# A two-stage Fourier filter and a gated MLP on one core: another order of loads and work in the first batch

## The chip, the cores and the metric

The kernel runs on one core of one Trainium2 chip. The metric is the device time of one execution in microseconds (us). The time before is the median of nine executions. One execution was also recorded by the hardware profiler; "the page" is the summary of that record, and "the trace" is the record itself.

## The reference

```python
def _attn_ref(x, filt_r, filt_i):            # x: (8, 3008, 256)
    X = np.fft.rfft(x, axis=1)
    F = (filt_r + 1j * filt_i)[None, :, :]   # filters: (1505, 256)
    return np.fft.irfft(X * F, n=x.shape[1], axis=1)

def _moe_ref(x, w_in, w_out, beta):          # x: (24064, 256)
    h = x @ w_in                             # w_in: (256, 2048)
    g = h * (1.0 / (1.0 + np.exp(-beta * h)))
    return g @ w_out                         # w_out: (2048, 256)
```

The output of the first part, 8 sequences of 3008 rows, is the input of the second, 24,064 tokens. Inputs and output are float32; the kernel multiplies in bf16.

## The kernel before

**The transform as matmuls.** The length S = 3008 is split as 47 x 64 (N1 = 47, M = 64). A forward transform is two matmul stages with a twiddle between them folded into the second table: table t1 (94 x 96) for the first, t2 (128 partitions x 24 frequencies k x 128) for the second. NK = 24, and each k stands for 64 frequencies (m) and, by symmetry, two rows of real and imaginary part. The inverse uses t3 (128 x 24 x 192, built from t2 by transposes, its last 64 columns negated) and t4 (t1 transposed). All tables are made on the chip from counting patterns (iota) and the sine function of ScalarE. The filters lie in fr_sb and fi_sb, 128 partitions x 24 x 256 in float32: row m of k on partition m and once more on partition 64 + m, so that a whole 128-partition product can be formed.

**The filters' way in.** `load_filters` (L86 to 91) is called for six groups of KU = 4 frequencies. Each call issues four loads on SP's queue of 128 KB each: fr for the first 32 rows (H = 32), fr for the last 32 (these are read backwards in the array), then fi for the same two. fr goes to partitions 64 to 127, fi to partitions 0 to 63. The 24 loads stand behind a two-element load `seen` (L310), which waits for a piece of t2, so that they do not start ahead of the first batch's input x0. `spread` (L470 to 473) then copies, on GpSimd (POOL), one group's fr and fi to the other 64 partitions.

**The first batch** is done ahead of everything, with functions of its own and an order written by hand at L303 to 345 and L475 to 531; the calls follow each other in each engine's queue as they are written:

- `s1_0` (L245) is the first stage with t1, `a0_turn` (L271) transposes its result for one group (it is evacuated by ScalarE or VectorE), `t2_half` and `t2_shift` (L222, L232) fill t2's halves, `t3_part` and `t3_neg` (L288, L294) fill one of three parts of t3, and `spin` (L267) issues matmuls whose result nobody reads.
- `s2_0(u)` (L426) is the second stage for group u: four matmuls into one PSUM buffer of two banks, then two products on VectorE, with fr_sb (L434) and with the sign rot and fi_sb (L435), to the tiles pq0 and pq1 (128 x 1024 bf16, two buffers each).
- `unit(u)` (L459) multiplies the products of group u by t3 (`s3_0`, L439) and lets ScalarE evacuate into zT. Group 5 goes by `s3_0` and `z_evac` to both engines.
- `z_turn`, `f4`, `f4_head`, `f4_tail` (L396 to 420) are turns of zT and the last stage with t4, which give y; here only for the first 512 tokens. The rest comes later, inside the MLP (`z_late`, `f_late`, L630 and L633).

All two-bank PSUM buffers of this part come from one pool of three.

**POOL's queue at this point** (L475 to 486) is, in this order: four spreads, the load of win_sb (the 1 MB of input weights, converted to bf16 on the way, one DMA), two spreads, the four loads of batch 1's input (xg, `load_x`), two scalings of output weights (`scale_wout`, L373). SP's queue has the filter loads and then the first two loads of output weights (ws, `load_wout`, L365).

**The MLP** (L751 to 791) runs 752 steps, 47 blocks of 512 tokens by 16 pieces of 128 hidden columns. A step issues two matmuls with win_sb into hps (L761), the Silu on ScalarE (L770), whatever a plan has put at this step (`at`, L642), and the four output matmuls of two steps earlier (L779). The plan (L663 to 711) spreads the transforms of batches 1 to 7 over the steps. For batch 1 it begins at once: `z_late` at steps 0 and 1, the sixteen first-stage pieces from step 0 on, two every three steps, each with a matmul on xg (L552), `f_late` for the second 512 tokens of batch 0 at steps 11, 11, 12 and 13, and the load of the stage's result (`a2_load`) at step 13.

Of the kernel before, what the change touches and what calls it, by code (L numbers as in the profile page):

```python
# [10 lines left out]
P = 128  # L11
# [25 lines left out]
def kernel(  # L37
# [45 lines left out]
    WZ = KP * J  # L83
    CH = M * J

    def load_filters(k0, k1):  # L86
        n = k1 - k0
        for filt, dst, p0 in ((filt_r, fr_sb, M), (filt_i, fi_sb, 0)):
            for q0, off, sg in ((p0, k0, 1), (p0 + H, N1 - k0, -1)):
                src = AP(filt.tensor, filt.offset + off * D, [[N1 * D, H], [sg * D, n], [1, D]])  # L90
                nc.sync.dma_start(dst[q0 : q0 + H, k0:k1, :], src)  # L91

    t1 = consts.tile([NP, KP], BF16, name="t1", tag="t1")
    t4 = consts.tile([KP, NP], BF16, name="t4", tag="t4")
# [46 lines left out]
    def iota(tile_, pattern, base=0, ch=0):  # L141
        nc.gpsimd.iota(tile_, pattern=pattern, base=base, channel_multiplier=ch)
# [39 lines left out]
    iota(kc[:], [[1, NK], [0, 2]])  # L182
    iota(cc[:], [[0, NK], [1, 2]], base=1)
    load_x0(8, 16)
    iota(vi[:, :, :H], [[1, NK], [N1, H]])
    load_x0(16, 24)
    iota(vi[:, :, H:], [[1, NK], [-N1, H]], base=N1 * (M - 1))
    load_x0(24, 28)
    make_identity(nc, ident)
    load_x0(28, 32)  # L190
# [2 lines left out]
    def shift_and(name, sh, mask, eng=None):  # L193
        t = small(name, I32)
        eng = eng or nc.vector
        if sh:
            eng.tensor_scalar(t[:], ip[:], sh, mask, ALU.logical_shift_right, ALU.bitwise_and)
        else:
            eng.tensor_scalar(t[:], ip[:], mask, None, ALU.bitwise_and)
        return t  # L200

    def affine(name, src, mul, add, eng=None):
        t = small(name)
        (eng or nc.vector).tensor_scalar(t[:], src[:], mul, add, ALU.mult, ALU.add)
        return t
# [10 lines left out]
    ms = affine("ms", shift_and("m_i", 0, M - 1), TURN / S, 0.0)  # L216
    off = affine("off", c_i, -TURN / 4, TURN / 4)
    q_i = shift_and("q_i", 0, 1)
    v_i = shift_and("v_i", 5, 1)
    q_p = (affine("q0", q_i, -1.0, 1.0), affine("q1", q_i, 1.0, 0.0))  # L220

    def t2_half(hi):  # L222
        t = sq.tile([P, NK, H], I32, name="u", tag=f"u{hi}")
        nc.vector.tensor_scalar(  # L224
            t[:], vi[:, :, hi * H : (hi + 1) * H], ms[:], off[:], ALU.mult, ALU.add
        )
        fold(t[:])
        nc.scalar.activation(
            t2[:, :, hi * H : (hi + 1) * H], t[:], ACT.Sin, scale=TWO_PI / TURN
        )  # L230

    def t2_shift(hi):  # L232
        for c in range(2):
            d0, s0 = (0, M) if c == 0 else (M, 0)
            dst = t2[d0 : d0 + M, :, M + hi * H : M + (hi + 1) * H]
            src = t2[s0 : s0 + M, :, hi * H : (hi + 1) * H]
            if c == hi:
                nc.vector.tensor_scalar_mul(dst, src, -1.0)
            else:
                nc.vector.tensor_copy(dst, src)  # L240

    MG = 4
    aTv = aT[:].rearrange("p e k (g m) -> p g e k m", m=MG)
# [20 lines left out]

    idle = tpsum.tile([P, 512], F32, name="tps", tag="tps")

    def spin(n):  # L267
        for _ in range(n):
            nc.tensor.matmul(idle[:], lhsT=rest[:, :P], rhs=rest[:], start=True, stop=True)

# [23 lines left out]
    def t3_neg(g, on_act):  # L294
        ks = slice(g * KH, (g + 1) * KH)
        evac(t3[:, ks, P:], t3[:, ks, :M], on_act, -1.0)
# [3 lines left out]
        nc.tensor.transpose(tp[:KP, 0, :NP], t1[:], ident[:NP, :NP])  # L300
        nc.scalar.activation(t4[:], tp[:KP, 0, :NP], ACT.Copy)

    spin(15)  # L303
    t1v = t1[:].rearrange("p (k q) -> p k q", q=2)
    for q in range(2):
        nc.scalar.activation(t1v[:, :, q], sn[:NP], ACT.Copy, scale=q_p[q][:NP])
# [1 line left out]
    t2_half(1)  # L308
    seen = sp.tile([1, 2], BF16, name="seen", tag="seen")
    nc.sync.dma_start(seen[:], t2[:1, 1, M - 2 : M])  # L310
    for u in range(NUN):
        load_filters(u * KU, (u + 1) * KU)
    gp = nc.gpsimd
    rot = affine("rot", v_i, 2.0, -1.0, gp)
    tiny = sp.tile([P, NFB], F32, name="tiny", tag="tiny")
    gp.tensor_tensor(tiny[:], beta_sb[:], beta_sb[:], ALU.mult)
    gp.tensor_scalar(tiny[:], tiny[:], 1e-12, 2e-6, ALU.is_lt, ALU.mult)
    gp.tensor_tensor(beta_sb[:], tiny[:], beta_sb[:], ALU.add)
    s1_0(0, (False,))
    s1_0(1, (True,))  # L320
    spin(5)
    t2_shift(0)
    t2_shift(1)
    nc.vector.memset(t2[:, 0, M : P : M - 1], 0.0)
    nc.scalar.activation(warm[:], ms[:], ACT.Silu)
    s1_0(2, (False,))
    s1_0(3, (True,))
    turn_t4()
    nc.gpsimd.tensor_scalar(t4[0:4], t4[0:4], 0.5, None, ALU.mult)
    spin(5)  # L330
    s1_0(4, (False,))
    s1_0(5, (True,))
    t3_part(0, True)
    s1_0(6, (False,))
    spin(2)
    s1_0(7, (False, True))
    spin(2)
    a0_turn(0, [turn8(), bank2([P, KH, P], BF16)], (False, True))
    a0_turn(1)
    t3_neg(0, False)  # L340
# [19 lines left out]
    def load_x(b, g):  # L360
        t = xpool.tile([KP, JG, D], BF16, name="xg", tag="xg")
        load_rows(t[:], b, g * JG, (g + 1) * JG)
        xg[b, g] = t
# [59 lines left out]
    r_p0 = ExitStack()  # L423
    p0pool = rpool("p0pool", r_p0, bufs=2, **tw)

    def s2_0(u):  # L426
        ps = bank2([P, KU, D])
        for i in range(KU):
            k1 = u * KU + i
            nc.tensor.matmul(ps[:, i, :], lhsT=t2[:, k1, :], rhs=a0[:, k1, :], start=True, stop=True)  # L430
        ks = slice(u * KU, (u + 1) * KU)
        for c in range(2):
            pq[u, c] = p0pool.tile([P, KU, D], BF16, name="pq_t", tag=f"pq{c}")
        nc.vector.tensor_tensor(pq[u, 0][:], ps[:], fr_sb[:, ks, :], ALU.mult)  # L434
        nc.vector.scalar_tensor_tensor(  # L435
            pq[u, 1][:], ps[:], rot[:], fi_sb[:, ks, :], ALU.mult, ALU.mult
        )
# [32 lines left out]
    def spread(u):  # L470
        ks = slice(u * KU, (u + 1) * KU)
        nc.gpsimd.tensor_copy(fr_sb[:M, ks, :], fr_sb[M:, ks, :])  # L472
        nc.gpsimd.tensor_copy(fi_sb[M:, ks, :], fi_sb[:M, ks, :])  # L473

    for u in range(4):  # L475
        spread(u)
    nc.gpsimd.dma_start(win_sb[:], moe_w_in.rearrange("(dc p) f -> p dc f", p=P))
    spread(4)
    spread(5)
    for g in range(4):  # L480
        load_x(1, g)
    load_wout(0)
    load_wout(WG)
    scale_wout(0)
    scale_wout(WG)

    s2_0(0)
    a0_turn(2)
    s2_0(1)
    unit(0)  # L490
    t3_part(1, True)
    t3_neg(1, True)
    a0_turn(3)
    s2_0(2)
    unit(1)
    a0_turn(4)
    s2_0(3)
    unit(2)
    a0_turn(5)
    t3_part(2, True)  # L500
    t3_neg(2, True)
    s2_0(4)
    unit(3)
    s2_0(5)
    unit(4)
    banks.close()

# [14 lines left out]
    for e in range(NDC):  # L522
        for h in range(2):
            pool, tag = (lps, "lp") if e else (fps, "fp")
            ps = pool.tile([P, 4, P], F32, name="fp", tag=tag)
            f4(0, h, e, ps)
            f4_head(0, h, e, ps, h == 1)
            late.append((0, h, e, ps))
    for a in late:
        f4_tail(*a, False)  # L530
    tail.close()
# [131 lines left out]
    for b in range(1, B):  # L663
        o = first_step[b - 1]
        if b == 1:
            at(0, z_late, 1, 0)
            at(1, z_late, 1, 1)
            s1_steps(1, range(16), [(2 * i + 1) // 3 for i in range(16)], False, (1, 4, 7, 10, 13))
            for i, r in enumerate((11, 11, 12, 13)):
                at(r, f_late, 1, i // 2, i % 2)  # L670
            for g in range(NG):
                at(o + 13, a2_load, 1, g)
            for hh, z0, f0 in ((2, (13, 14), (15, 16, 17, 18)), (3, (18, 19), (20, 21, 22, 23))):
                for e in range(NDC):
                    at(z0[e], z_late, hh, e)
                for i, r in enumerate(f0):
                    at(r, f_late, hh, i // 2, i % 2)
            s23_steps(1, [o + r for r in (22, 24, 26, 28, 30, 34, 36, 38, 40, 42, 44, 46)], 5, 1)
            for h in range(J // JG):
                at(o + 54, zz_load, 1, h)  # L680
            s4_steps(1, [o + 66 + (i * 12) // 15 for i in range(16)], 2)
            for f in (2, 3):
                at(f, load_wout, f * WG)
                at(f, scale_wout, f * WG)
            if B > 2:
                for g in range(4):
                    at(o + 24 + 3 * g, load_x, 2, g)
                late = (54, 55, 56, 57, 58, 59, 60, 61, 66, 67, 68, 70, 72, 73, 74, 76)
                s1_steps(2, range(16), [o + r for r in late], False)
                for g in range(NG):  # L690
                    at(o + 80, a2_load, 2, g)
                if B > 3:
                    for g in range(4):
                        at(o + (62, 68, 88, 92)[g], load_x, 3, g)
            continue
        base = [o + 16 * n + s for n in range(4) for s in (4, 8, 12)]
        if b == 2:
            base[:6] = [o + r for r in (8, 12, 19, 22, 26, 29)]
        s23_steps(b, base, 6, False)
        for h in range(J // JG):  # L700
            at(o + 70, zz_load, b, h)
        s4_steps(b, [o + 80 + (i * 13) // 15 for i in range(16)], False)
        if b + 1 < B:
            early = [o + 16 * n + s for n in range(4) for s in (7, 13)]
            late = [o + s for s in (66, 67, 69, 70, 72, 73, 75, 76)]
            s1_steps(b + 1, range(16), early + late, False)
            for g in range(NG):
                at(o + 82, a2_load, b + 1, g)
            if b + 2 < B:
                for g in range(4):  # L710
                    at(o + (30, 62, 88, 92)[g], load_x, b + 2, g)
# [108 lines left out]
```

## Time and profile before

| | us |
|---|---|
| median of nine executions | 783.02 |
| lowest and highest | 782.28, 784.27 |
| the profiled execution | 782.77 |
| its span in the record | 781.0 |
| TensorE busy (share) | 768.3 (98%) |
| ScalarE busy (share) | 552.5 (71%) |
| VectorE busy (share) | 446.5 (57%) |
| POOL busy (share) | 151.0 (19%) |

The profiled execution's own time is 1.77 us above its span, which begins with the first and ends with the last recorded instruction. PE is TensorE, PEld its weight loads, DVE VectorE, ACT ScalarE, SP SyncE. L434 is line 434 of the kernel. In a row of a timeline the first number is the time from the span's start, the second the duration, then engine, line, operation, and written and read tiles with partitions x elements and type; a bracket tells how long the engine stood idle before it and what it waited for. In the chain of waits each row is one step of the chain that ended last. The row of digits shows the busy share in tenths for forty equal slices of the span, 19.5 us each.

### The profile page before, as it was taken

The numbers are of one execution on the slowest core, as the hardware profiler recorded it, in microseconds if no ns is written. First come the engines' busy times: TensorE is split into PE (matmuls) and PEld (weight loads), VectorE is DVE, ScalarE is ACT, GpSimd is POOL, SyncE is SP. The second block draws the span as 40 slices with busy tenths as digits, with TensorE's granted clock in tenths as the row PEclk, the third lists the DMA queues.
The fourth block names the chain that finished last, engine by engine and source line by source line (L and its number), as shares of the span: only waits on it lengthen the run. The fifth ranks groups of instructions, "written<-read, shape, count | busy, mean of one in ns | idle before, by whom it ended". The sixth has DMA issues, their size and how long they took to land.

```text
span 781.0 us, 15238 instructions
## 1 busy us (share of the span) xinstructions
PE 768.3 (98%) x6046; PEld 543.3 (70%) x6046; DVE 446.5 (57%) x713; ACT 552.5 (71%) x814; POOL 151.0 (19%) x154
## 2 busy tenths in 40 slices
PE   8799999999999999999999999999999999999997
PEld 5567767766776667866678666776667776776665
DVE  8869754866556665566646665567655666321001
ACT  6767867666677766777667776677666777777776
POOL 6714400322012220122201322022200222000000
PEclk9999999999999999999999999999999999999999
DMA  9975575244912358042671417622164111500101
GB/s 185 236 225 98 150 204 156 68 104 122 256 39 76 107 111 247 29 106 77 139 220 40 125 48 180 177 75 68 49 189 135 48 48 48 157 28 28 55 28 55
DMA packets 84139, 88.51 MB, mean 113 GB/s; under 512 B 5772, under 2 KB 74380, under 8 KB 84068
## 3 DMA queue, kind: packets, MB, share of 16 engines
q1 hardware_dynamic: 79892, 73.81, 31.6%
q0 software_dynamic: 4032, 13.60, 10.3%
q8 instruction: 47, 0.77, 0.4%
q14 instruction: 24, 0.20, 0.1%
q10 hardware_dynamic: 144, 0.13, 0.0%
HBM read 54.47 MB, written 46.66 MB: 129 GB/s over the span
## 4 chain that ended last, share of the span: by engine, by line
PE 95%; DMA 2%; POOL 1%; DVE 1%; issue 1%; SPq 0%; ACT 0%; DVEq 0%; POOLq 0%
PE acc L779 42%; PE hps L761 42%; PE ps L552 3%; PE ps L620 2%; PE ps L598 2%; PE ps L568 2%; DMA xg<-in_x_dram 1%; DMA fr_sb<-in_filt_r_dram 1%; POOL fi_sb L473 1%; POOL fr_sb L472 1%; PE tp L400 0%; SPq L91 0%; PE ps L405 0%; DVE u L224 0%; DVE u L145 0%
## 5 line engine op out<-in xcount | busy, mean ns | idle before, releaser
L770 ACT ACTIVATE gT<-hps,beta_sb 128x512 bf16<-128x512 f32 x752 | 516.9, 687 | 213.9 <-PE hps L761 212.2
L779 PE MATMUL acc<-wout_sb,gT 128*128 128x256 bf16 x3008 | 453.0, 272 | 0.0
L761 PE MATMUL hps<-y,win_sb 128*128 128x512 bf16 (+7 forms) x1728 | 447.9, 351 | 0.6 <-DMA win_sb<-in_moe_w_in_dram 0.6
L779 PEld LDWEIGHTS <-gT 128*128 128x128 bf16 x3008 | 286.8, 98 | 121.9 <-issue 1.4
L587 POOL TENSOR_TENSOR yh<-a_t,b_t 128x512 bf16<-128x512 f32 x84 | 106.5, 1268 | 422.9 <-DVE b_t L586 421.6
L761 PEld LDWEIGHTS <-win_sb 128*128 128x128 bf16 x1728 | 164.8, 98 | 25.0 <-DMA win_sb<-in_moe_w_in_dram 0.8
L112 DVE COPY ost<-acc 128x512 f32<-128x512 f32 (+1 forms) x94 | 60.0, 680 | 138.3 <-PE acc L779 138.2
L112 DVE CAST a<-ps 96x512 bf16<-96x512 f32 x107 | 72.9, 685 | 52.7 <-PE ps L552 48.7
L114 DVE TENSOR_SCALAR y<-ps 128x376 bf16<-128x376 f32 (+2 forms) x128 | 63.2, 510 | 61.5 <-PE ps L620 57.9
L582 DVE TENSOR_TENSOR a_t<-ps,fr_sb 128x512 f32<-128x512 f32 x84 | 58.1, 692 | 67.0 <-PE ps L568 66.5
L583 DVE SCALAR_TENSOR_TENSOR b_t<-ps,fi_sb 64x512 f32<-64x512 f32 x84 | 58.2, 693 | 1.1
L586 DVE TENSOR_TENSOR b_t<-ps,fi_sb 64x512 f32<-64x512 f32 x84 | 57.4, 683 | 1.1
L112 DVE CAST z<-ps 128x512 bf16<-128x512 f32 x72 | 49.3, 685 | 1.7 <-PE ps L598 0.8
L620 PEld LDWEIGHTS <-zz 96*128 96x128 bf16 x448 | 29.7, 97 | 22.9
L552 PE MATMUL ps<-xg,t 94*96 94x512 bf16 x112 | 42.0, 382 | 0.8 <-DMA xg<-in_x_dram 0.8
L620 PE MATMUL ps<-t,zz 96*128 96x94 bf16 x448 | 34.7, 205 | 0.0
L598 PE MATMUL ps<-yh,t 128*128 128x256 bf16 x168 | 32.1, 273 | 0.0
L568 PE MATMUL ps<-a,t 128*128 128x256 bf16 x168 | 32.1, 273 | 0.0
L598 PEld LDWEIGHTS <-t 128*128 128x128 bf16 x168 | 16.2, 98 | 17.7 <-issue 0.7
L568 PEld LDWEIGHTS <-t 128*128 128x128 bf16 x168 | 16.1, 98 | 16.3
L171 POOL DMA_DIRECT2D xg<-in_x_dram x24 | 12.5, 521 | 56.7 <-PE ps L552 56.7
L552 PEld LDWEIGHTS <-t 94*96 94x96 bf16 x112 | 13.7, 123 | 11.0 <-DMA xg<-in_x_dram 0.9
(94 smaller groups left out, 175.2 us busy)
## 6 DMA issues: line engine op xcount, KB each, us to landing
out_dram<-ost SPq DMA_DIRECT2D x42, 512.0 KB, 3.0
d<-a SPq DMA_DIRECT2D x28, 384.0 KB, 5.2
a<-d SPq DMA_DIRECT2D x28, 384.0 KB, 5.0
d<-z SPq DMA_DIRECT2D x28, 384.0 KB, 3.7
zz<-d SPq DMA_DIRECT2D x28, 384.0 KB, 6.8
xg<-in_x_dram POOLq DMA_DIRECT2D x24, 384.0 KB, 6.2
out_dram<-ost SPq DMA_DIRECT2D x9, 256.0 KB, 3.5
ws<-in_moe_w_out_dram SPq DMA_DIRECT2D x4, 512.0 KB, 6.2
```

The lines of the kernel that those rows point to most:

```text
L112: nc.vector.tensor_copy(dst, src)
L114: nc.vector.tensor_scalar_mul(dst, src, scale)
L552: nc.tensor.matmul(ps[:KP], lhsT=t1[:], rhs=xg[b, g][:NP, jj : jj + 2, :], start=True, stop=True)
L568: nc.tensor.matmul(ps[:, e, :], lhsT=t2[:, k0 + e, :], rhs=st["a2", b, g][:, kk + e, :], start=True, stop=True,)
L582: nc.vector.tensor_tensor(a_t[:], ps[:], fr_sb[:, ks, :], ALU.mult)
L583: nc.vector.scalar_tensor_tensor(b_t[:M], ps[M:], -1.0, fi_sb[M:, ks, :], ALU.mult, ALU.mult)
L587: nc.gpsimd.tensor_tensor(yh[:], a_t[:], b_t[:], ALU.add)
L598: nc.tensor.matmul(ps[:, e, :], lhsT=t3[:, 2 * i + e, :P], rhs=yh[:, e, :], start=True, stop=True)
L620: nc.tensor.matmul(ps[:, e, :NP], lhsT=zz[:, j0 % JG + e, dc * P : (dc + 1) * P], rhs=t4[:], start=True, stop=True,)
L761: nc.tensor.matmul(hps[:, pos - t0 : pos - t0 + ln], lhsT=win_sb[:, dc, fb * P : (fb + 1) * P], rhs=ys[b][:, dc, n0 : n0 + ln], start=(dc ...
L770: nc.scalar.activation(gT[:], hps[:], ACT.Silu, scale=beta_sb[:, fb : fb + 1])
L779: nc.tensor.matmul(acc_of(i, tb)[:, tb % 2, :], lhsT=blk[i * NFB + fb][:, tb * P : (tb + 1) * P], rhs=wout_sb[:, fb, :], start=(fb == 0 an ...
```

## The change

It touches only what happens before the MLP and in its first steps.

- **Filters.** The first and last 32 rows are no longer put side by side in each half of 64 partitions but alternately (even and odd partitions), in the filters and in the columns of t2 (and so of t3). Loads alternate between fr and fi. For k below 16 (DUP) there are 16 loads of 128 KB as before; for k from 16 to 23 there are four loads of 256 KB to the usual halves and four more of 256 KB to the other halves, straight from HBM. The spreads of groups 4 and 5 are gone.
- **Table t2.** Its second 64 columns were made by four operations (two copies, two negations); now by two exclusive-or operations on pairs of bf16 read as int32, which flip the sign of one of the pair. The sign rot comes from the lowest bit of the partition index, not from bit 5; v_i is gone.
- **Group 4's second product** is made on POOL: ScalarE copies the PSUM result, scaled with rot, to zc (float32), and `pool_product` multiplies it with fi_sb in two operations of 128 x 512.
- **Input weights** come in two loads, columns 0 to 511 and the rest, and the first load of xg follows at once. The other three and the two scalings of output weights follow `pool_product(4)` in POOL's queue.
- **Order by hand.** The second part of t3 moves ahead of `unit(0)`, the turns of groups 4 and 5 ahead of `unit(1)` and of `s2_0(4)`, `s2_0(4)` ahead of `unit(2)`, `s2_0(5)` ahead of `unit(3)`. Three idle matmuls are added before `unit(3)`, two before the `f4_tail`s.
- **Plan.** Batch 1's first stage comes two steps later, its `a2_load` one step later, and `f_late` of the second 512 tokens at steps 2 to 5.

```diff
-    def load_filters(k0, k1):
-        n = k1 - k0
-        for filt, dst, p0 in ((filt_r, fr_sb, M), (filt_i, fi_sb, 0)):
-            for q0, off, sg in ((p0, k0, 1), (p0 + H, N1 - k0, -1)):
-                src = AP(filt.tensor, filt.offset + off * D, [[N1 * D, H], [sg * D, n], [1, D]])
-                nc.sync.dma_start(dst[q0 : q0 + H, k0:k1, :], src)
+    FILTERS = ((filt_r, fr_sb), (filt_i, fi_sb))
+    DUP = 2 * KH
+
+    def load_filters(k0, k1, halves):
+        for hi, off, sg in ((0, k0, 1), (1, N1 - k0, -1)):
+            for (filt, dst), p0 in zip(FILTERS, halves):
+                src = AP(filt.tensor, filt.offset + off * D, [[N1 * D, H], [sg * D, k1 - k0], [1, D]])
+                nc.sync.dma_start(dst[p0 + hi : p0 + M : 2, k0:k1, :], src)
...
-    v_i = shift_and("v_i", 5, 1)
...
-    def t2_shift(hi):
-        for c in range(2):
+    def t2_shift():
+        pairs = t2[:].rearrange("p k m -> p (k m)").bitcast(I32).rearrange("p (k m) -> p k m", k=NK)
+        for c, bit in enumerate((1 << 15, -(1 << 31))):
             d0, s0 = (0, M) if c == 0 else (M, 0)
-            dst = t2[d0 : d0 + M, :, M + hi * H : M + (hi + 1) * H]
-            src = t2[s0 : s0 + M, :, hi * H : (hi + 1) * H]
-            if c == hi:
-                nc.vector.tensor_scalar_mul(dst, src, -1.0)
-            else:
-                nc.vector.tensor_copy(dst, src)
+            nc.vector.tensor_scalar(
+                pairs[d0 : d0 + M, :, H:], pairs[s0 : s0 + M, :, :H], bit, None, ALU.bitwise_xor
+            )
...
-    for u in range(NUN):
-        load_filters(u * KU, (u + 1) * KU)
+    for u in range(DUP // KU):
+        load_filters(u * KU, (u + 1) * KU, (M, 0))
+    load_filters(DUP, NK, (M, 0))
+    load_filters(DUP, NK, (0, M))
     gp = nc.gpsimd
-    rot = affine("rot", v_i, 2.0, -1.0, gp)
+    rot = affine("rot", q_i, 2.0, -1.0, gp)
...
-    def s2_0(u):
+    zc = sr.tile([P, KU, D], F32, name="zc", tag="zc")
+
+    def s2_0(u, on_pool=False):
...
+        if on_pool:
+            nc.scalar.activation(zc[:], ps[:], ACT.Copy, scale=rot[:])
         nc.vector.tensor_tensor(pq[u, 0][:], ps[:], fr_sb[:, ks, :], ALU.mult)
+        if on_pool:
+            return
         nc.vector.scalar_tensor_tensor(
             pq[u, 1][:], ps[:], rot[:], fi_sb[:, ks, :], ALU.mult, ALU.mult
         )
...
+    def load_win(f0, f1):
+        nc.gpsimd.dma_start(
+            win_sb[:, :, f0:f1], moe_w_in[:, f0:f1].rearrange("(dc p) f -> p dc f", p=P)
+        )
+
     for u in range(4):
         spread(u)
-    nc.gpsimd.dma_start(win_sb[:], moe_w_in.rearrange("(dc p) f -> p dc f", p=P))
-    spread(4)
-    spread(5)
-    for g in range(4):
-        load_x(1, g)
+    load_win(0, 4 * P)
+    load_win(4 * P, FF)
+    load_x(1, 0)
+
+    def pool_product(u):
+        for i in range(0, KU, 2):
+            k0 = u * KU + i
+            nc.gpsimd.tensor_tensor(
+                pq[u, 1][:, i : i + 2, :], zc[:, i : i + 2, :], fi_sb[:, k0 : k0 + 2, :], ALU.mult
+            )
+
     load_wout(0)
     load_wout(WG)
-    scale_wout(0)
-    scale_wout(WG)
 
     s2_0(0)
     a0_turn(2)
     s2_0(1)
-    unit(0)
     t3_part(1, True)
     t3_neg(1, True)
+    unit(0)
     a0_turn(3)
     s2_0(2)
+    a0_turn(4)
     unit(1)
-    a0_turn(4)
     s2_0(3)
+    a0_turn(5)
+    s2_0(4, True)
+    pool_product(4)
+    for g in range(1, 4):
+        load_x(1, g)
+    scale_wout(0)
+    scale_wout(WG)
     unit(2)
-    a0_turn(5)
     t3_part(2, True)
     t3_neg(2, True)
-    s2_0(4)
+    s2_0(5)
+    idle = tpsum.tile([P, 512], F32, name="tps", tag="tps")
+    spin(3, idle)
     unit(3)
-    s2_0(5)
     unit(4)
...
+    spin(2, zps.tile([P, 512], F32, name="zp", tag="zp"))
     for a in late:
         f4_tail(*a, False)
...
-            s1_steps(1, range(16), [(2 * i + 1) // 3 for i in range(16)], False, (1, 4, 7, 10, 13))
-            for i, r in enumerate((11, 11, 12, 13)):
+            s1_steps(1, range(16), [2 + (2 * i + 1) // 3 for i in range(16)], False, (1, 4, 7, 10, 13))
+            for i, r in enumerate((2, 3, 4, 5)):
                 at(r, f_late, 1, i // 2, i % 2)
             for g in range(NG):
-                at(o + 13, a2_load, 1, g)
+                at(o + 14, a2_load, 1, g)
```

More of the change, by code (lines that the diff above doesn't have):

```diff
@@ L184 @@
     load_x0(8, 16)
-    iota(vi[:, :, :H], [[1, NK], [N1, H]])
+    viv = vi[:].rearrange("p k (m h) -> p k m h", h=2)
+    iota(viv[:, :, :, 0], [[1, NK], [N1, H]])
     load_x0(16, 24)
-    iota(vi[:, :, H:], [[1, NK], [-N1, H]], base=N1 * (M - 1))
+    iota(viv[:, :, :, 1], [[1, NK], [-N1, H]], base=N1 * (M - 1))
     load_x0(24, 28)
@@ L224, in t2_half @@
         nc.vector.tensor_scalar(
-            t[:], vi[:, :, hi * H : (hi + 1) * H], ms[:], off[:], ALU.mult, ALU.add
+            t[:], viv[:, :, :, hi], ms[:], off[:], ALU.mult, ALU.add
         )
@@ L228, in t2_half @@
         nc.scalar.activation(
-            t2[:, :, hi * H : (hi + 1) * H], t[:], ACT.Sin, scale=TWO_PI / TURN
-        )
-    def t2_shift(hi):
-        for c in range(2):
+            t2[:, :, :M].rearrange("p k (m h) -> p k m h", h=2)[:, :, :, hi],
+            t[:],
+            ACT.Sin,
+            scale=TWO_PI / TURN
+        )
+    def t2_shift():
+        pairs = t2[:].rearrange("p k m -> p (k m)").bitcast(I32).rearrange("p (k m) -> p k m", k=NK)
+        for c, bit in enumerate((1 << 15, -(1 << 31))):
             d0, s0 = (0, M) if c == 0 else (M, 0)
-            dst = t2[d0 : d0 + M, :, M + hi * H : M + (hi + 1) * H]
-            src = t2[s0 : s0 + M, :, hi * H : (hi + 1) * H]
-            if c == hi:
-                nc.vector.tensor_scalar_mul(dst, src, -1.0)
-            else:
-                nc.vector.tensor_copy(dst, src)
+            nc.vector.tensor_scalar(
+                pairs[d0 : d0 + M, :, H:], pairs[s0 : s0 + M, :, :H], bit, None, ALU.bitwise_xor
+            )
     MG = 4
@@ L265, with spin @@
     idle = tpsum.tile([P, 512], F32, name="tps", tag="tps")
-    def spin(n):
+    def spin(n, idle):
         for _ in range(n):
@@ L301, in turn_t4 @@
         nc.scalar.activation(t4[:], tp[:KP, 0, :NP], ACT.Copy)
-    spin(15)
+    spin(15, idle)
     t1v = t1[:].rearrange("p (k q) -> p k q", q=2)
@@ L320 @@
     s1_0(1, (True,))
-    spin(5)
-    t2_shift(0)
-    t2_shift(1)
+    spin(5, idle)
+    t2_shift()
     nc.vector.memset(t2[:, 0, M : P : M - 1], 0.0)
@@ L329 @@
     nc.gpsimd.tensor_scalar(t4[0:4], t4[0:4], 0.5, None, ALU.mult)
-    spin(5)
+    spin(5, idle)
     s1_0(4, (False,))
@@ L334 @@
     s1_0(6, (False,))
-    spin(2)
+    spin(2, idle)
     s1_0(7, (False, True))
-    spin(2)
+    spin(2, idle)
     a0_turn(0, [turn8(), bank2([P, KH, P], BF16)], (False, True))
```

## The prediction

> **What bounds the kernel now.** I read the page first: parts 1 and 2 for the busy shares, then the chain of waits cut to the first 40 us, then each engine's timeline there, then the stages of equal kind.
>
> ```profile
> PE 768.3 (98%) x6046; PEld 543.3 (70%) x6046; DVE 446.5 (57%) x713; ACT 552.5 (71%) x814; POOL 151.0 (19%) x154
> PE   8799999999999999999999999999999999999997
> DMA  9975575244912358042671417622164111500101
> ```
>
> TensorE is busy 98% of the span; from 62 to 400 us it is busy in all 338 us. The change adds no useful matmul and removes none. So only the idle time of the start can be won or lost, and the first slices show where: TensorE at 8 and 7 tenths, the DMA engines at 9.
>
> ```profile
> 11.58 4.81 DMA fr_sb<-in_filt_r_dram
> ...
> 22.08 1.04 POOL fi_sb L473
> ...
> 27.25 0.98 POOL fi_sb L473
> 28.23 7.83 DMA xg<-in_x_dram
> 36.07 0.04 issue
> 36.11 0.42 PE ps L552
> ```
>
> The chain runs from filter loads over the copies of the filters to the other partitions (POOL) to the load of batch 1 (xg). Beside it runs the frequency product on VectorE:
>
> ```profile
> 15.88 1.22 DVE L434 TENSOR_TENSOR pq_t<-sps,fr_sb 128x1024 bf16<-128x1024 f32 x1
> ...
> 29.43 1.27 DVE L435 SCALAR_TENSOR_TENSOR pq_t<-sps,rot,fi_sb 128x1024 bf16<-128x1024 f32 x1
> ```
>
> Twelve such operations fill 15.88 to 30.70 us with 0.6 us of gaps. After them: the last inverse matmuls (to 31.38 us), evacuation, turns, and the first MLP matmul.
>
> ```profile
> 34.27 0.61 PE L761 MATMUL hps<-y,win_sb 128*128 128x512 bf16 x2 [0.61 <-DMA win_sb<-in_moe_w_in_dram]
> 34.71 0.61 PE L400 MATMUL tp<-ident,y 128*128 128x128 bf16 x8
> 36.11 0.42 PE L552 MATMUL ps<-xg,t 94*96 94x512 bf16 x1 [0.79 <-DMA xg<-in_x_dram]
> ```
>
> Its data would have allowed about 34.1 us (ScalarE's last evacuation of y ends at 34.08). Then 0.79 us is lost on xg. I count the start as 34.27 + 0.79 = 35.06 us: after that TensorE hardly stops until the very end. Two chains thus end within a microsecond: VectorE's product, and the DMA queue. The stages show the second one:
>
> ```profile
> 12.50:22.50 10.00, 8.02 (x107) 6.22 (x104) 9.29 (x11) 7.43 (x11) 7.68 (x8) 1.00 1.05 233
> 25.50:27.50 2.00, 1.70 (x24) 1.47 (x22) 1.72 (x3) 1.97 (x4) 1.88 (x3) 1.00 1.10 342
> 28.50:36.00 7.50, 5.30 (x74) 4.12 (x73) 5.87 (x13) 4.67 (x9) 4.08 (x6) 1.00 1.06 214
> ```
>
> The last three columns are clock, DMA share and GB/s. The engines are full throughout. While filters alone move they carry 233 GB/s; the 128-partition output weights (ws) carry 342.
>
> [...] win_sb, issued on POOL at 23.07, lands only 11.2 us later, behind filters and ws. [...]
>
> **The change part by part.**
>
> *Early VectorE and POOL edits.* Four shifts of the second table (8.35 to 9.81 us) become two integer ones; the nearest row, the 128x768 int32 fold, takes 0.56 us, so 1.12 for 1.46. One 0.06 us operation goes. Table writes and reads become strided: between 0 and 0.3 us more per operation. All lie under ScalarE's table load (9.05 to 10.33) and under x0's load, which lands at 12.1. I take 0; without that cover it would be 0.3 us either way.
>
> *ScalarE's order.* The second inverse table moves ahead of the first unit's evacuation, and turns 4 and 5 move up. This fills ScalarE's idle 1.72 us before 19.01 and frees TensorE's waits of 0.83 and 0.32 us before 24; of them 0.32 + 0.28 us reach VectorE. Gain 0.6 us.
>
> *Group 4's second product* leaves VectorE (1.20 us by start-to-start). ScalarE copies it out scaled [...] into its idle time near 24; POOL multiplies: two 128x512 operations at 1.27 us (L587's row) = 2.54 us. Alone, the two parts let VectorE end at 29.45: the last group must also wait for unit 3 to free its buffer. So 1.25 us is to be had, and a start near 32.9 with an early xg.
>
> *Filters.* POOL's copies of groups 4 and 5 (four of 1.04 us) go; k 16 to 23 is now loaded from HBM for both halves: eight loads of 256 KB instead of eight of 128 KB, 1.05 MB more, behind the first sixteen on SP's queue. Before, the sixteenth landed at about 21.9 us, and landings follow each other by 0.57 us per 128 KB. At that pace the last of the eight lands at 21.9 + 8 x 1.13 = 30.9 us. VectorE wants group 4's filters at 25.2. **Here the cover is gone**: formerly POOL produced these halves without the full DMA engines.
>
> The new order alternates fr [...] and fi [...], so the pace may rise. Lower bound: none. Upper bound: ws's 342 GB/s, 0.38 us per 128 KB, but SP issues one per 0.45: 21.9 - 15 x 0.12 + 8 x 0.77 = 26.2. I take 0.50 us for the first sixteen, [...] and 1.10 us for each large load, whose run on one half is as long as a pair's before: 21.9 - 15 x 0.07 + 8 x 1.10 = 29.7 us.
>
> Who waits: group 4's first product and, for its buffer, group 5's; POOL's product; behind it in POOL's queue three loads of xg and the output-weight scaling (1.9 us each, wanted two steps into the MLP, thus hidden); TensorE, in order, at unit 3. From the last landing: product 2.54, unit 4's second half 0.45 + 0.1, last inverse 1.05, then 2.75 us as before (31.38 to about 34.1), 0.15 for waits: start = landing + 7.0.
>
> *Weights in two pieces.* win_sb's first quarter now suffices for four steps: it removes the 0.61 us wait, of which 0.2 was real. Its load and xg still queue behind the filters. xg landed at 36.07, 9.5 us after the last filter (26.6); it is now wanted two steps later (2.2 us after the start). So start is at least landing + 9.5 - 2.2 = landing + 7.3, a little less where win_sb gets past ws.
>
> *Fill and MLP order.* Five idle matmuls fall into waits: 0. Four late inverse pieces move to steps 2 to 5 and batch 1's first transform two steps later; the same matmuls, VectorE then 1.3 us per step of about 1.4. I take 0, at most 0.5 us.
>
> *Sum.* Break-even is a landing near 27.9 us. At 29.7: start = 36.9, against 35.06: +1.85 us. The profiled execution took 782.77 us with a span of 781.0, 1.77 around it; the median of nine is 783.02, 0.25 above. 782.77 + 1.85 + 0.25 gives 784.9.
>
> **Rivals.**
> A, forecast (0.55): the pace hardly rises, landing 29.2 to 30.9, start 36.2 to 38.2: 784.1 to 786.1.
> B (0.26): [...] landing 26.8 to 29.2; the gain on VectorE is given back by xg: start 34.0 to 36.2: 782.0 to 784.1, about no change. [...]
> C, the other side (0.13): [...] landing 26.2. VectorE is the bound again; start 33.0 to 33.5, 781.0 to 781.5. It decides from landings before 26.3, a pace above about 320 GB/s.
> D (0.06): TensorE stays idle from about 26.6 past 30 us and its clock, 1.00 until now, falls for the tail of the batch [...]. Its stretch of about 2 us of tail matmuls at half speed: a further 1 to 2 us, 786.1 to 787.5.
>
> **How the numbers follow.** A change of 0.2%, 1.6 us, is about the least that a measurement of this kernel can tell from none: below 781.45 is faster, above 784.6 slower. Of A four fifths lie above it, 0.44; with D slower is 0.50. B and the rest of A, 0.37, are within it; C gives 0.13 faster. The range leaves out D's end and C's best: 781.6 to 786.8.
>
> **What would show it.** In the profile after: fr_sb and fi_sb landings (their last near 29.7) and GB/s between 12 and 28 us (240 to 260, not 300); VectorE idle some 3 us before its fifth product, with a DMA as releaser; POOL's product after it; TensorE idle before unit 3; the first MLP matmul near 36.9. Right whatever the pace: no VectorE gap before 25, no wait on win_sb. Filter landings before 27.9 would make the forecast wrong, and so would xg overtaking the filters.

## The result and the profile after

The kernel after takes 793.96 us (median of 10, 790.61 to 794.87), against 783.10 us for the kernel before (median of 32 with the runs beside it). The ratio is 1.0132, with a 95% interval from 1.0122 to 1.0143; the medians differ by 10.9 us. The forecast was 784.9 us, in a range up to 786.8. The sign was right; the size was between five and six times too small.

The page's busy shares and slices, in the same order as those of before above (PEclk is the clock granted to TensorE, in tenths of its full speed):

```profile
PE 771.5 (97%) x6051; PEld 546.4 (69%) x6051; DVE 444.8 (56%) x709; ACT 554.0 (70%) x815; POOL 149.9 (19%) x153
PE   8389999999999999999999999999999999999997
PEclk9889999999999999999999999999999999999999
DMA  7965665541851329313482234803154211500101
```

Before, every slice was at 9 tenths or more:

```profile
PEclk9999999999999999999999999999999999999999
```

TensorE's second slice (19.8 to 39.7 us) falls from 7 tenths to 3, and the granted clock drops there too. Past 60 us almost nothing is lost or won: each Silu from the 15th step to the last starts 12.57 or 12.58 us later than before. So the loss is made ahead of the MLP, as predicted. The chain of waits, cut to this stretch:

```profile
24.65 0.62 SPq L93
25.31 13.97 DMA fi_sb<-in_filt_i_dram
39.59 0.10 issue
39.68 2.50 POOL pq_t L499 x2
...
42.22 0.82 PE sps L454 x6
43.05 1.71 PE lp L454 x16
44.75 1.83 PE zp L404 x16
...
48.15 0.59 PE hps L788 x2
```

One filter load, the last, issued at 25.31 us, took 14 us; behind it are POOL's product, unit 4, the last inverse stage and the first MLP matmul at 48.15. This work between the last filter and the MLP is called the tail below. On VectorE:

```profile
24.52 1.28 DVE L445 SCALAR_TENSOR_TENSOR pq_t<-sps,rot,fi_sb 128x1024 bf16<-128x1024 f32 x1
34.91 2.36 DVE L442 TENSOR_TENSOR pq_t<-sps,fr_sb 128x1024 bf16<-128x1024 f32 x2 [9.12 <-DMA fr_sb<-in_filt_r_dram]
```

The gap ahead of group 4's first product, forecast at 3 us, is 9.12. The stages of equal kind (clock, DMA share and GB/s are the last three columns):

```profile
12.50:22.50 10.00, 9.05 (x127) 7.51 (x125) 8.45 (x11) 9.04 (x12) 6.42 (x7) 1.00 0.69 194
28.50:36.00 7.50, 0.00 (x0) 0.00 (x0) 1.09 (x1) 0.74 (x1) 0.00 (x0) 0.82 1.09 228
36.00:40.00 4.00, 1.03 (x8) 0.77 (x8) 1.81 (x3) 0.00 (x0) 0.32 (x1) 0.50 1.05 317
```

This is the first surprise: while filters alone move, the engines carry 194 GB/s, less than the 233 of before, and are busy only 0.69 of the time. They are no longer the limit. SP's queue is: its loads now follow each other with 0.04 us between them, and each takes longer to issue (lowest, median and highest duration in ns). Before:

```profile
L91 SPq DMA_DIRECT2D fi_sb<-in_filt_i_dram x12: 311/422/436, 10.0 to 22.0; - x12
```

and after:

```profile
L93 SPq DMA_DIRECT2D fi_sb<-in_filt_i_dram x12: 588/600/619, 10.2 to 25.3; - x12
```

A load to every other partition takes SP 0.60 us to issue instead of 0.42, whether it carries 128 or 256 KB. The last of the 24 loads thus leaves at 25.31 us instead of 21.98, and that is behind the first weights, which POOL issued at 24.39. What this leads to is seen in the DMA queues from 31 to 36 us (q0 is POOL's, q1 SP's; packets, MB, share of 16 engines):

```profile
q0 software_dynamic: 293, 0.87, 87.5%
q1 hardware_dynamic: 296, 0.29, 20.8%
```

The two queues move the same number of packets. But nearly all of POOL's packets (win_sb, xg) hold 3 or 4 KB here (268 of the 293), and the filter rows that are read backwards come in packets of 1 KB (280 of SP's 296). The output weights, which stand behind the filters on SP's queue, have next to no part in this yet: by the landing marks in the trace, the first of the 16 DMA engines is done with the last filter load at 35.9 us. So the filters, on which everything waits, get 0.29 MB in 5 us, 58 GB/s, and the weights, which nobody needs yet, three times that.

### The profile page after: what moved, and what is told of

The parts are those of the page before. It is cut to its first block, busy times and chain, and to the rows that moved or that the text cites. A ratio compares the mean times of both kernels' runs of the same rounds, so it can differ in the third digit from the quotient of the medians.

```text
span 793.0 us, 15243 instructions
## 1 busy us (share of the span) xinstructions
PE 771.5 (97%) x6051; PEld 546.4 (69%) x6051; DVE 444.8 (56%) x709; ACT 554.0 (70%) x815; POOL 149.9 (19%) x153
## 4 chain that ended last, share of the span: by engine, by line
PE 94%; SPq 2%; DMA 2%; DVE 1%; POOL 0%; issue 0%; ACT 0%; POOLq 0%
PE acc L806 42%; PE hps L788 41%; PE ps L579 3%; PE ps L647 2%; PE ps L595 2%; PE ps L625 2%; SPq L93 2%; DMA fi_sb<-in_filt_i_dram 2%; PE tp L404 0%; POOL pq_t L499 0%; PE ps L409 0%; PE zp L404 0%; PE lp L454 0%; DVE u L226 0%; DVE u L147 0%
## 5 line engine op out<-in xcount | busy, mean ns | idle before, releaser
L647 PEld LDWEIGHTS <-zz 96*128 96x128 bf16 x448 | 29.7, 97 | 22.9
L579 PEld LDWEIGHTS <-t 94*96 94x96 bf16 x112 | 13.8, 123 | 10.4
```

The source lines that it names most:

```text
L579: nc.tensor.matmul(ps[:KP], lhsT=t1[:], rhs=xg[b, g][:NP, jj : jj + 2, :], start=True, stop=True)
L647: nc.tensor.matmul(ps[:, e, :NP], lhsT=zz[:, j0 % JG + e, dc * P : (dc + 1) * P], rhs=t4[:], start=True, stop=True,)
```

## The experiments

Theory after the result: three things in a row make the loss. (1) The interleaved rows slow SP's issue. (2) The last filters then share the engines with the weights, equal in packets and not in bytes (296 and 293 from 31 to 36 us). (3) TensorE's clock falls in the gap (0.50 from 36 to 40 us). Rivals: it is the added volume alone; the engines' pace was the limit anyway; the tail is longer for another reason. All ratios are to the kernel before, timed beside the run on the same chip. Its own median there was 783.3 to 783.8 us, so a difference of two medians from different groups of runs can be off by about half a microsecond.

**One part undone at a time.** The rows side by side again (with t2's columns, its four operations and rot), the rest as after:

```diff
-                nc.sync.dma_start(dst[p0 + hi : p0 + M : 2, k0:k1, :], src)
+                nc.sync.dma_start(dst[p0 + hi * H : p0 + (hi + 1) * H, k0:k1, :], src)
```

> The kernel after, with only the interleaving of rows undone (rows, columns of t2 and the sign rot as before; fr and fi still alternate, k from 16 on is still loaded twice). Theory of the issue: a load that goes to every other partition costs SP 0.65 us instead of about 0.45, so here SP issues a load every 0.45 to 0.5 us, the sixteenth filter load lands near 20.5 instead of 22.9 us, the last filter at 35 to 38 instead of 39.3, the MLP starts 1.5 to 4 us earlier, 790 to 792.5 us. Rival (the alternation is what makes SP slow, or the engines are the limit anyway): 0.6 us or more per load as in the kernel after, 793.5 to 794.5 us.

Measured: 787.08 us, ratio 1.0038 (1.0025 to 1.0051). SP issues at 0.43 us a load, the last at 21.62. The 23rd load lands at 29.2 (34.6 in the kernel after); POOL's product, waiting for the 24th, starts at 32.4 (39.7). The issue theory holds. Its price is 6.9 us, more than the 1.5 to 4 us that I expected; most of the filters are now also out of the weights' way, which I take to be the reason.

The second loading undone, the interleaving kept:

```diff
-    for u in range(DUP // KU):
-        load_filters(u * KU, (u + 1) * KU, (M, 0))
-    load_filters(DUP, NK, (M, 0))
-    load_filters(DUP, NK, (0, M))
+    for u in range(NUN):
+        load_filters(u * KU, (u + 1) * KU, (M, 0))
...
     load_x(1, 0)
+    spread(4)
+    spread(5)
```

> The kernel after, with only the second loading of k 16 to 23 undone: 24 loads of 128 KB in the new order and layout, and POOL copies groups 4 and 5 as before (after it has issued the two pieces of win_sb and xg). Theory of the sharing: the filters are all issued by 25.3 us and land by 28.5, before the weights move at 28.5; last copy near 30, POOL's product to 32.5, MLP from 35 to 36, clock 1.00 throughout, 782.5 to 784 us. Rival (the slow last loads come from the 0.65 us issue or from 1 KB packets alone): last filter past 31 us, start past 38, over 786 us.

Measured: 791.39 us, ratio 1.0099 (1.0078 to 1.0121). My expectation failed: 1 MB less to load brought only 2.6 us. POOL's queue shows why:

```profile
24.12 1.57 POOL L484 DMA_DIRECT2D win_sb<-in_moe_w_in_dram  x2
25.67 0.57 POOL L173 DMA_DIRECT2D xg<-in_x_dram  x1
26.28 1.04 POOL L480 COPY fr_sb<-fr_sb 64x1024 f32<-64x1024 f32 x1
27.37 1.04 POOL L481 COPY fi_sb<-fi_sb 64x1024 f32<-64x1024 f32 x1
30.21 1.04 POOL L480 COPY fr_sb<-fr_sb 64x1024 f32<-64x1024 f32 x1 [1.80 <-DMA fr_sb<-in_filt_r_dram]
34.61 1.03 POOL L481 COPY fi_sb<-fi_sb 64x1024 f32<-64x1024 f32 x1 [3.36 <-DMA fi_sb<-in_filt_i_dram]
```

The last two filters leave SP at 24.25 and 24.91 us, just after the weights (24.12). The engines, almost a third idle (share 0.71 from 22.5 to 25.5 us), take up the weights' packets 1.6 us after their issue, not 4 us as in the kernel after; so even two loads of 128 KB need until 30.2 and 34.5 us. From 28.5 to 30 us POOL's queue moves 133 packets and SP's 17, so here the last filter does not even get an equal number. With the rows interleaved, the volume is not the point; what stands behind the weights is. (With the rows side by side the volume does cost, as the combination further down shows.)

**The weights out of the way.** Both pieces of win_sb and the first xg behind POOL's product:

```diff
     for u in range(4):
         spread(u)
-    load_win(0, 4 * P)
-    load_win(4 * P, FF)
-    load_x(1, 0)
...
     pool_product(4)
+    load_win(0, 4 * P)
+    load_win(4 * P, FF)
+    load_x(1, 0)
```

> The kernel after, with only the place of three loads in POOL's queue changed: both pieces of win_sb and the first xg stand behind POOL's product, so that they cannot move beside the filters. Theory of the sharing [...]: the last filter lands at 32 to 33.5 instead of 39.3, POOL's product ends near 36, unit 4 follows; the first piece of win_sb lands near 39, MLP from 40.5 to 42, 785.5 to 788.5 us. Rival (volume and pace of SP's queue alone): last filter at 37 or later, start at 46 or later, 792 us or more, since the weights are late as well.

Measured: 794.29 us, ratio 1.0131 (1.0114 to 1.0148). The time is the rival's, the mechanism the theory's. POOL's product starts at 33.2 us, and the first MLP matmul at 41.3 instead of 48.15; but the weights are now too late, and the first matmul on xg waits:

```profile
47.89 0.58 PE L579 MATMUL ps<-xg,t 94*96 94x512 bf16 x1 [4.20 <-DMA xg<-in_x_dram]
```

What was won on the filters is paid back on xg. To see the first effect without the second, the weights are only held back by about 2 us, with two copies of 1.04 us that nothing reads:

```diff
+    pad = sr.tile([P, KU, D], F32, name="pad", tag="pad")
...
     for u in range(4):
         spread(u)
+    for _ in range(2):
+        nc.gpsimd.tensor_copy(pad[:M], fr_sb[M:, 3 * KU : 4 * KU, :])
     load_win(0, 4 * P)
```

> The kernel after with two copies of 1.04 us into a tile that nothing reads, on POOL ahead of the weights: win_sb and xg are issued at about 26.5 us instead of 24.4, after SP has issued its last filter (25.3). Nothing else differs. Theory of the order of issue: the last filters are not shared any more and land near 33 instead of 39.3 us, the MLP starts at 41.5 to 43, xg waits a little, 786.5 to 789.5 us: 2 us of delay gain 5 to 7. Rival (they share whenever both have something to move, whoever was first): last filter at 37 to 39.3 again, 792.5 to 795 us.

Measured: 789.61 us, ratio 1.0076 (1.0063 to 1.0090). Useless work of 2.1 us in POOL's queue makes the kernel 4.35 us faster. POOL's queue:

```profile
24.21 2.14 POOL L494 COPY pad<-fr_sb 64x1024 f32<-64x1024 f32 x2
26.30 1.57 POOL L487 DMA_DIRECT2D win_sb<-in_moe_w_in_dram  x2
27.84 0.57 POOL L173 DMA_DIRECT2D xg<-in_x_dram  x1
33.86 2.49 POOL L502 TENSOR_TENSOR pq_t<-zc,fi_sb 128x512 bf16<-128x512 f32 x2 [5.45 <-DVE pq_t L443]
```

POOL's product starts at 33.9 instead of 39.7 us. The bracket names VectorE, whose product ended 0.2 us before; but the last filter landed at 33.46, 0.40 us before, and that is its distance in the kernel after too (39.28 and 39.68). So POOL still starts right behind the last filter; the filter is what comes earlier. Here the order of issue decides. The time lies just above my range, for a reason that I had not named: the MLP starts at 41.70 us, as expected, but then TensorE waits for the output weights, which stand behind the filters on SP's queue:

```profile
51.05 0.60 PE L809 MATMUL acc<-wout_sb,gT 128*128 128x256 bf16 x4 [1.32 <-POOL wout_sb L378]
```

**The interleaving by itself**, in the kernel before (t2's columns, its exclusive-or operations and rot with it):

```diff
-            for q0, off, sg in ((p0, k0, 1), (p0 + H, N1 - k0, -1)):
+            for q0, off, sg in ((p0, k0, 1), (p0 + 1, N1 - k0, -1)):
...
-                nc.sync.dma_start(dst[q0 : q0 + H, k0:k1, :], src)
+                nc.sync.dma_start(dst[q0 : p0 + M : 2, k0:k1, :], src)
```

> The kernel before, with only the interleaving of rows (every other partition in the filter loads, in t2's columns, the two exclusive-or operations, rot from the lowest bit); order and number of loads as before. Theory of the issue: SP takes 0.6 to 0.65 us per load instead of 0.42 to 0.47, so the last of the 24 is issued near 25 us instead of 22, behind POOL's weights (issued at 23 to 24.5)[...]: last filter past 31 us instead of 26.6, MLP start at 40 to 46, 787 to 792 us. Rival (the engines, at 233 GB/s, were the limit and hide SP's issue): last filter at 26.6 to 27.5, 782.5 to 784.5 us.

Measured: 788.48 us, ratio 1.0062 (1.0048 to 1.0076): about 5 us, without any added byte. SP takes 0.61 us a load, the last one leaves at 25.05 us behind the weights (23.89), and POOL's last copy starts at 34.9 instead of 27.3. The rival (the engines at 233 GB/s hide SP) falls.

**The clock.** Idle matmuls in the gap, first 45 ahead of unit 3:

```diff
-    spin(3, idle)
+    spin(45, idle)
     unit(3)
```

> The kernel after, with 45 idle matmuls instead of 3 ahead of unit 3, which fill TensorE from 27 to about 37 us and leave no other work later. Theory of the clock: TensorE's clock stays at 1.00, the tail from the last filter (39.3) to the MLP takes 7.0 us instead of 8.8 and the first steps run at full speed, minus 1.5 to 2.5 us: 791.5 to 792.5 us. Rival (the tail is longer for another reason, such as the weights): no change, 793.5 to 794.5.

Measured: 793.38 us, ratio 1.0114 (1.0088 to 1.0139). This lies just below the rival's range, and the interval takes in the kernel after's ratio, so the time shows nothing. The trace shows more: the clock was 1.00 until 40 us and fell to 0.72 on average from 40 to 46, where TensorE had three waits of 0.9 to 1.1 us around unit 4. So 12 more were put there:

```diff
     unit(3)
+    spin(12, idle)
     unit(4)
```

> The kernel after with 45 idle matmuls instead of 3 ahead of unit 3 and 12 more ahead of unit 4 (which waits for POOL's product from about 38 to 41 us), since in the run with 45 alone the clock still fell behind unit 3. Theory of the clock: 1.00 from 28 to 48 us, the tail from POOL's first product (39.7) to the MLP takes 6.9 to 7.2 us instead of 8.5, and the median is 1.5 to 2.2 us below the kernel after: 791.8 to 792.5. Rival (the tail is that long at full clock): 793.4 to 794.

Measured: 792.62 us, ratio 1.0104 (1.0084 to 1.0125), 1.3 us below the kernel after and just above my range. That is little against the noise (the two intervals still touch), so the traces have to show it. From the kernel after, the stretch behind the gap,

```profile
40.00:46.00 6.00, 4.17 (x37) 3.71 (x38) 1.83 (x4) 1.92 (x4) 6.00 (x7) 0.50 0.50 86
```

and from this one:

```profile
40.00:46.00 6.00, 4.30 (x63) 3.33 (x62) 3.04 (x10) 3.37 (x7) 6.00 (x7) 1.00 0.64 114
```

At half clock 4.17 us of TensorE time did 37 matmuls, at full clock 4.30 us did 63, the next stage's somewhat shorter ones among them. From the start of POOL's product to the MLP it takes 7.0 us (38.78 to 45.79) instead of 8.5 (39.68 to 48.15). So the rival falls.

**Both costly parts undone**: rows side by side and copies by POOL, with POOL's product kept.

> The kernel after with two of its parts undone together: rows side by side again, and groups 4 and 5 copied by POOL instead of loaded twice; fr and fi still alternate, and ScalarE's order, POOL's product, the weights in two pieces and the plan stay. Theory of the order of issue (a filter load that SP issues before POOL issues the weights runs at full pace[...]): SP issues the last filter near 20.7 us, before the weights at about 23; last filter lands at 25 to 26; POOL copies until 29 and multiplies until 31.5, DVE ends near 31; MLP from 35.5 to 36.5, span 780.8 to 782, median within 1 us of the kernel before. Rival (undoing one part brought 7 us, undoing the other 2.5, and they simply add up: 793.96 - 6.9 - 2.6): 784.5 us, 1.5 above the kernel before.

Measured: 784.29 us, ratio 1.0010 (1.0002 to 1.0019). This is 0.8 us above the kernel before of its group (783.45), within the theory's 1 us, but also close to the rival's figure, so the time doesn't part the two. The trace does: the last filter leaves at 21.10, ahead of the weights at 23.33, and lands at 25.0, as the theory said. POOL copies until 29.8 and multiplies until 32.4, each 0.8 to 0.9 us later than expected. And one thing was not foreseen: the clock averages 0.65 from 28.5 to 36 us, so the tail is longer, and the MLP starts at 38.2 instead of 36. In addition, group 4's second product back on VectorE:

```diff
-    s2_0(4, True)
-    pool_product(4)
+    s2_0(4)
```

> As the run with both parts undone, and in addition group 4's second product is back on DVE (no copy zc, nothing on POOL behind the copies). If POOL, whose copies end near 29, sets the end there: DVE ends near 30.5, MLP from 33.2 to 34.2, 0.5 to 1.5 us below the kernel before (781.6 to 782.6 us on its median of 783.1), and 1.5 to 2.5 below the run with POOL's product. Rival (moving a product to POOL is free or a gain): same as or slower than the run with it.

Measured: 781.11 us, ratio 0.9969 (0.9958 to 0.9980). This is a little better than expected. This version beats both kernels, by about 2 us the kernel before. VectorE's last product ends at 30.9 us; in the run below with the weights alone changed it ends at 31.5, which agrees with the 0.6 us that the prediction gave ScalarE's new order, though the two runs differ in the order of the filter loads too. POOL's product cost 3.2 us here: it stands behind POOL's copies, and the clock falls with it (1.00 from 28.5 to 36 us in this run, 0.65 in the one before). TensorE's start of the MLP has no wait left:

```profile
33.68 0.38 PE L275 MATMUL zp<-rest 128*128 128x512 bf16 x1
34.12 0.59 PE L791 MATMUL hps<-y,win_sb 128*128 128x512 bf16 x2
34.55 0.61 PE L406 MATMUL tp<-ident,y 128*128 128x128 bf16 x8
...
36.35 0.38 PE L582 MATMUL ps<-xg,t 94*96 94x512 bf16 x1
```

The remaining combination, side by side and loaded twice, but the product on VectorE (both edits as above):

> The kernel after with the rows side by side and with group 4's second product on DVE, so that of its three costly parts only the double loading is left. The last filter as in the run with the rows alone undone (near 32), then one DVE product of 1.3 us, the last inverse matmuls and 2.8 to 3.5 us: MLP from 37 to 38.5, 783.3 to 785.3 us; 2 to 3.5 us less than with POOL's product, 2.5 to 4 more than without the double loading.

Measured: 786.74 us, ratio 1.0034 (1.0026 to 1.0042). This missed: with the double loading the product's place is worth only 0.3 us in the median, not 2 to 3.5. Against the run before it, the double loading costs 5.6 us. In the trace the MLP does start as expected, at 38.49 us against 40.99 with POOL's product. But the profiled execution (785.08) is the shortest of 20, so it doesn't show what the median waits for; why the two costs don't add stays open.

So of the three costly parts, each taken alone, the interleaving costs about 5 us (in the kernel before), the double loading 5.6 and POOL's product 3.2 (both on the fastest version, 781.11); these make 13.8, and from the fastest version to the kernel after it is 12.9 us.

**What gained.** The kernel before with win_sb in two pieces, xg behind them and the new plan:

```diff
-    nc.gpsimd.dma_start(win_sb[:], moe_w_in.rearrange("(dc p) f -> p dc f", p=P))
+    load_win(0, 4 * P)
+    load_win(4 * P, FF)
+    load_x(1, 0)
     spread(4)
     spread(5)
-    for g in range(4):
+    for g in range(1, 4):
         load_x(1, g)
```

> The kernel before with three edits of the change alone: win_sb in two pieces, the first xg right behind them in POOL's queue (ahead of the copies of groups 4 and 5), and the plan of the first MLP steps. If the 2.3 us that the run with neither interleaving nor double loads nor POOL's product gained on the kernel before come from the two waits at the start of the MLP (0.61 on win_sb, 0.79 on xg): no wait on either, DVE's last product 0.3 to 1 us later for the longer issue on POOL, 781.5 to 782.5 us on the median of before of 783.1. Rival (the gain is that of ScalarE's order and of the alternation): 782.8 to 784.

Measured: 781.81 us, ratio 0.9977 (0.9969 to 0.9985). Neither wait is left; VectorE's last product ends 0.8 us later (31.5), as POOL's issue of two more loads delays the copies. And the kernel before with only the order of loads changed:

```diff
-        for filt, dst, p0 in ((filt_r, fr_sb, M), (filt_i, fi_sb, 0)):
-            for q0, off, sg in ((p0, k0, 1), (p0 + H, N1 - k0, -1)):
+        for hi, off, sg in ((0, k0, 1), (1, N1 - k0, -1)):
+            for filt, dst, p0 in ((filt_r, fr_sb, M), (filt_i, fi_sb, 0)):
+                q0 = p0 + hi * H
```

> The kernel before with one edit: the filter loads alternate between fr and fi (rows side by side). The engines are then less than full in the filter phase (packets of 4 KB take 160 ns instead of 296) and SP's issue, 0.47 us a load, sets the pace: last filter near 24.7 to 25.5 instead of 26.6 us, 250 GB/s or more from 12.5 to 22.5. DVE is the bound beside it, xg lands up to 1 us earlier: 782.2 to 783.2 us, at most 0.9 below the kernel before. Rival (the alternation does nothing by itself): 233 GB/s, 26.6, 783.1.

Measured: 782.80 us, ratio 0.9988 (0.9980 to 0.9996). Its filter phase, to be set against 1.04 to 1.05 and 233 of before:

```profile
12.50:22.50 10.00, 8.22 (x109) 6.23 (x106) 9.33 (x12) 7.48 (x10) 7.47 (x8) 1.00 0.85 252
```

More bytes with less engine time: a packet of 4 KB takes 159 ns in the median (208 in the mean) instead of 296 (294). Alternation does free the engines; with rows side by side SP can use it. The gain in time is small, 0.5 to 0.9 us.

## Why the prediction was wrong

It was right in where (the filters of groups 4 and 5, "Here the cover is gone"), in who waits (VectorE's fifth product, POOL's product, TensorE at unit 3) and in the sign, which was not luck, since the double loading, from which it followed, does cost time with the rows side by side as well. POOL's product (2.49 us, forecast 2.54) had the right price, and ScalarE's scaled copy took 1.15 us; there is no VectorE gap before 25 us between its products (0.56 us ahead of the first) and no wait on win_sb. The start of the MLP, 48.15 instead of 36.9 us, is 11.25 us off, by these steps:

- **"SP issues one per 0.45".** This step failed first. The price was taken from loads to adjacent partitions and used for loads to every other one. Measured 0.65 a load with its gap: the sixteenth lands near 22.9 (the fifteenth's 22.3 and one issue more) instead of 20.9, about 2 us. (The 0.50 us a load behind the 20.9 was my estimate; nothing in the traces of before showed what the alternation does.) The interleaved write was priced on VectorE ("0.3 us more per operation"; measured, its two folds took 0.61 and 0.71 us instead of 0.56) and not on the queue that issues it, and "engines are full" hid that the change would make another part the limit.
- **Eight large loads at 1.10 us.** Without sharing (weights behind the product) they took from about 22.3 to at most 33.2 us: up to 1.36 each, some 2 us in all.
- **"Its load and xg still queue behind the filters".** This is the step that failed most: about 6 us, the difference between 39.7 and the 33.2 to 33.9 us of the two runs in which the weights were issued later. They queued behind in the kernel before because they were issued after the last filter (23.07 against 21.98), not because of a rule. The prediction named the sign of this error (xg overtaking filters) and gave it no time: the first piece of win_sb landed at 32.4 us, ahead of the last two filters (34.6 and 39.3). Two things made it so long. One is the sharing: from 31 to 36 us the queues moved 293 packets against 296, and with 3 or 4 KB on one side and 1 KB on the other, equal numbers are not equal bytes (0.87 against 0.29 MB); how the engines choose between the queues the trace doesn't show. The other is when a load's first packet moves, and there the order of issue counted: with the weights 2 us later, none of their packets moved for 6.1 us, while SP's queue still had the filters.
- **The clock as a rival of its own (D, 0.06).** It belonged into the forecast with the gap: from 28.5 to 36 us the clock averaged 0.60 to 0.82 in every run whose tail came late without the added idle matmuls, and 1.00 in the others. The tail took 8.5 us from the start of POOL's product instead of 7.0. The half speed in D was an assumption, since the clock of before was 1.00 in every stretch of the start; the kernel after then showed it (0.50 from 36 to 46 us). Its price of 1 to 2 us was right (1.3 in the median, 1.5 in the trace).

These make about 11.5 us, near the 11.25. The median missed the forecast by less, 9.1 us, for two reasons. The span grew by some 1.0 us less than the start of the MLP moved: 0.5 us lies in the first MLP steps (12.57 instead of 13.09), a gain where the text had allowed a loss of up to 0.5; the other 0.5 us lies after the last Silu, and no run explains it. And 1.1 us is the profiled execution itself, which lay 0.85 us above its median, where the one before lay 0.25 below. The forecast's chance for "slower", 0.50, was too low because rivals B and C, which made up most of the other half, asked only how fast the engines could go, which was an estimate in both.

## What to carry to other kernels

Before a load is given another shape, ask what issues it and what that costs per load (here 0.60 us instead of 0.42); a queue that hides behind full DMA engines can become the limit, as SP's did here, when they had a share of 0.69 instead of 1.05. Where two queues shared the engines from 31 to 36 us of the kernel after, they moved equal numbers of packets and not of bytes (293 and 296; 0.87 and 0.29 MB): what is urgent should be issued before bulk loads of another queue, and the gap between the two issue times (here 1.1 us in the kernel before) is a margin to be kept, as real as a wait. A move that empties TensorE can cost the clock besides: in the eight runs here in which TensorE stood idle for 2.8 us or more of the 7.5 from 28.5 to 36 us, the clock averaged 0.60 to 0.82 in this stretch; in the six others it was 1.00.

## What the runs showed of the hardware

- The weights' first packet came 1.5 to 1.7 us after POOL issued the load when the engines had room (runs with copies kept and rows interleaved, or with the queue empty), and later when SP's queue had a backlog: 2.9 to 3.4 us with 128 KB loads side by side and alternating, 4.2 in the kernels before and after, 6.0 to 6.3 with the weights 2 us later or with rows side by side and loaded twice. That the backlog is the cause was not tested by itself. It was not a strict order: with the rows alone undone, the last filter load left 1.6 us ahead of the weights and still shared its end with them.
- SP's issue time for a filter load went with the partitions written (0.42 us for 32 adjacent ones, 0.60 for every other one), not with size (128 or 256 KB).
- Two orders of the same 24 loads differ by 19 GB/s (233 and 252) and by almost a factor of two in the median time of a 4 KB packet (296 and 159 ns), less in the mean (294 and 208).
- Idle matmuls in a gap of 8 us kept TensorE's clock at 1.00 until three waits of 0.9 to 1.1 us followed each other (0.72 from 40 to 46 us); with these filled as well it stayed at 1.00.
